# A build-time order that lets buffers of rows sent by POOL be reused only after the landing, and that counts key-value products as traced

## Chip, cores, metric

One core of one Trainium2 chip. The metric is the device time of one execution in microseconds (us). A ratio is the mean time of one kernel's runs over the mean of the other's runs of the same rounds, so it is not quite the ratio of the medians that are quoted.

## The reference

Attention without softmax, then four experts; all float32.

```python
# q, k, v: (8, 8, 576, 64); x: (4608, 512); w1: (4, 512, 1024); w2: (4, 1024, 512)
kv  = np.einsum('bhsd,bhse->bhde', k, v)
out = np.einsum('bhsd,bhde->bhse', q, kv)
rms = np.sqrt(np.mean(out * out, axis=-1, keepdims=True) + 1e-06)
x   = (out / rms * g_norm)            # then (B,H,S,D) -> (B*S, H*D)
p   = domain_probs / (domain_probs.sum(-1, keepdims=True) + 1e-09)
for e in range(4):
    out += p[:, e:e+1] * (np.maximum(x @ w1[e], 0.0) @ w2[e])
```

## The kernel before

The kernel replaces large products by sums and fewer products (Strassen-like forms, two levels deep), so VectorE (DVE) and GpSimd (POOL) make many sums and differences in SBUF while TensorE (PE) multiplies. Rows are worked in 9 chunks for each of the 4 experts. ScalarE (ACT) and DVE take products out of PSUM.

The order of all instructions is made while the kernel is built. A greedy planner holds a model of the time that each operation takes and fills five engines and a stock of buffers ("slots"; the kind "big" has 29, plus 4 that come free later). Each engine then executes its list in order.

```python
def ready(op, eng):                       # may op start on eng, and when
    for d in op.deps:
        when = max(when, d.end + (self.SAME if d.eng == eng else self.CROSS))  # 0.06, 0.3
    ...                                   # need: slots that its outputs want
    for k, n in need.items():
        if len(free[k]) < n + ...: return None
        when = max(when, sorted(free[k])[n - 1][0])
...
    op.start, op.eng = t, eng
    if eng == "SP":                       # loads and plain stores: the landing is counted
        busy[eng] = t + op.cost[eng]
        bus = max(bus, t + 1.5) + op.kb / 215.0
        op.end = bus + 0.5
        ...
    else:                                 # all others, POOL's sends too: over when issued
        op.end = busy[eng] = t + op.cost[eng]
    ...
    for b in op.outs:                     # a slot: the one that came free earliest
        if b.kind is not None and b.slot is None:
            free[b.kind].sort()
            b.slot = free[b.kind].pop(0)[1]
            ...
    for b in op.bufs:                     # the last user of b gives its slot back
        b.left -= 1
        if b.left == 0 and b.kind is not None:
            end = max(o.end for o in [op] + b.readers + b.writers) + self.CROSS
            free[b.kind].append((end, b.slot))
            ...
```

Slots hold the results of one chunk: two "big" buffers `acc`, the first for rows 0 and 1, the second for rows 2 and 3. For the experts after the first, POOL adds them into the output in HBM:

```python
def send(key, i):
    def fn(eng):
        for parts, dst in where:
            if e and not again:
                nc.gpsimd.dma_start(out=dst, in_=cell(i)[parts, :], accum_op=ALU.add)
            else:
                nc.sync.dma_start(out=dst, in_=cell(i)[parts, :])
    plan.add(key, {"POOL": 0.9 * len(where)} if e and not again else {"SP": ...},
             fn, ..., kb=256, holds=[acc[i // 2]])
```

The other users are sums and differences that DVE or POOL may take, whichever is free (`either`), among them the differences `ht` of hidden values that the inner products of a chunk read.

## Time and profile before

| | before |
|---|---|
| time, median of 3 runs | 1790.44 us (1790.4 to 1791.32) |
| traced execution | 1788.53 us, of which 1786.8 from first to last instruction |
| PE busy | 98% |
| idle PE: to 100 / 100 to 640 / 640 to 1715 us / after | 12.9 / 0 / 15.8 / 4.7 us |

How to read it: PE is the bound, so only what makes PE idle counts, and the stretch from 640 us on (experts 2 to 4, the ones that POOL sends) is where it can be helped. The prediction below shows the lines. One it does not show is the chain of work that ended last, by engine:

```profile
PE 85%; DMA 6%; POOL 4%; DVE 2%; issue 2%; SPq 0%; ACT 0%; DVEq 0%; POOLq 0%; ACTq 0%
```

Transfers and POOL hold a tenth of this chain although PE is 98% busy. The chain follows one releaser at a time and credits a transfer with time in which PE still worked.

### The profile page before, as it was taken

The numbers are of one execution on the slowest core, as the hardware profiler recorded it, in microseconds if no ns is written. First come the engines' busy times: TensorE is split into PE (matmuls) and PEld (weight loads), VectorE is DVE, ScalarE is ACT, GpSimd is POOL, SyncE is SP. The second block draws the span as 40 slices with busy tenths as digits, with TensorE's granted clock in tenths as the row PEclk, the third lists the DMA queues.
The fourth block names the chain that finished last, engine by engine and source line by source line (L and its number), as shares of the span: only waits on it lengthen the run. The fifth ranks groups of instructions, "written<-read, shape, count | busy, mean of one in ns | idle before, by whom it ended". The sixth has DMA issues, their size and how long they took to land.

```text
span 1786.8 us, 36290 instructions
## 1 busy us (share of the span) xinstructions
PE 1753.4 (98%) x14132; PEld 1677.8 (94%) x14132; DVE 1140.3 (64%) x1910; ACT 817.5 (46%) x1913; POOL 831.4 (47%) x815
## 2 busy tenths in 40 slices
PE   8899999999999999999999999999999999999998
PEld 8799999999999999999999999999999999999997
DVE  5755564555674667777674577777674577777654
ACT  3544544454343445544443345555543445544541
POOL 4854433444345434444455534444455634444520
PEclk9999999999999999999999999999999999999999
DMA  9744534441443334444464434444465434444441
GB/s 234 243 134 157 173 106 141 157 148 64 153 159 104 106 96 107 107 107 106 120 166 130 107 95 107 107 104 101 106 176 133 115 96 107 107 106 102 103 117 36
DMA packets 148587, 220.79 MB, mean 124 GB/s; under 512 B 49600, under 2 KB 90816, under 8 KB 148416
## 3 DMA queue, kind: packets, MB, share of 16 engines
q1 hardware_dynamic: 133312, 191.21, 33.7%
q0 software_dynamic: 15104, 27.27, 10.7%
q8 instruction: 111, 1.82, 0.4%
q14 instruction: 60, 0.49, 0.1%
HBM read 145.30 MB, written 73.14 MB: 122 GB/s over the span
## 4 chain that ended last, share of the span: by engine, by line
PE 85%; DMA 6%; POOL 4%; DVE 2%; issue 2%; SPq 0%; ACT 0%; DVEq 0%; POOLq 0%; ACTq 0%
PE u L802 38%; PE db L966 18%; PE db L1039 9%; PE ab L1039 8%; PE ab L966 6%; DMA out_dram<-big 4%; POOL big L337 3%; DVE big L337 1%; PE ab L595 1%; PE ab L577 1%; PE ab L605 1%; POOL out_dram L936 1%; PE ab L562 1%; PE ab L644 0%; DMA out_dram<-small 0%
## 5 line engine op out<-in xcount | busy, mean ns | idle before, releaser
L802 PE MATMUL u<-xf,big 128*128 128x128 f32 x3600 | 503.0, 276 | 5.8 <-ACT snap L818 4.7
L826 DVE TENSOR_TENSOR big<-u,snap 128x256 f32<-128x256 f32 x720 | 298.7, 421 | 293.1 <-PE u L802 205.0
L802 PEld LDWEIGHTS u<-xf,big 128*128 128x128 f32 x3600 | 462.2, 192 | 17.1 <-ACT snap L818 7.5
L337 DVE TENSOR_TENSOR big<-big,big 128x1024 f32<-128x1024 f32 (+1 forms) x377 | 431.3, 1159 | 40.4 <-ACT big L785 15.6
L818 ACT ACTIVATE snap<-u 128x256 f32<-128x256 f32 x756 | 289.5, 384 | 362.1 <-PE u L802 263.8
L802 PE MATMUL u<-xf,w1y 128*128 128x128 f32 x2700 | 378.4, 275 | 0.0
L802 PEld LDWEIGHTS u<-xf,w1y 128*128 128x128 f32 x2700 | 340.4, 192 | 2.1
L337 POOL TENSOR_TENSOR big<-big,big 128x256 f32<-128x256 f32 (+1 forms) x174 | 238.3, 1374 | 151.7 <-DVE big L337 65.0
L966 PE MATMUL db<-big,big 128*128 128x256 f32 x1280 | 302.8, 380 | 0.0
L966 PEld LDWEIGHTS db<-big,big 128*128 128x128 f32 x1280 | 231.3, 190 | 25.3
L785 ACT ACTIVATE big<-big 128x1024 f32<-128x1024 f32 x131 | 138.0, 1053 | 38.5 <-DVE big L337 31.8
L818 ACT ACTIVATE big<-u 128x256 f32<-128x256 f32 x240 | 92.1, 384 | 114.6 <-PE u L802 106.8
L1064 ACT ACTIVATE snap<-db 128x256 f32<-128x256 f32 x216 | 76.6, 355 | 125.6 <-PE db L1039 115.3
L337 POOL TENSOR_TENSOR big<-big 128x512 f32<-128x512 f32 (+1 forms) x81 | 95.5, 1184 | 69.0 <-DVE big L337 54.1
L936 POOL DMA_DIRECT2D out_dram<-big x98 | 89.4, 973 | 68.9 <-ACT big L913 50.3
L1072 DVE TENSOR_TENSOR big<-ab,snap 128x256 f32<-128x256 f32 x216 | 83.2, 385 | 51.0 <-PE ab L1039 33.8
L1100 POOL TENSOR_TENSOR big<-big 128x512 f32<-128x512 f32 x21 | 29.6, 1411 | 174.7 <-DVE big L337 174.7
L913 ACT ACTIVATE big<-db,p_all 128x256 f32<-128x256 f32 x100 | 47.4, 474 | 131.5 <-PE db L966 131.5
L920 DVE SCALAR_TENSOR_TENSOR big<-db,p_all,big 128x256 f32<-128x256 f32 x83 | 40.0, 482 | 81.3 <-PE db L966 80.7
L337 POOL TENSOR_TENSOR small<-big,small 128x128 f32<-128x128 f32 (+1 forms) x46 | 28.8, 625 | 127.2 <-DVE big L337 68.0
L1039 PE MATMUL db<-big,big 128*128 128x128 f32 x616 | 86.3, 275 | 0.0
L1039 PE MATMUL ab<-kv,big 128*128 128x128 f32 x500 | 74.7, 278 | 10.1 <-DVE big L1072 10.1
(185 smaller groups left out, 2520.0 us busy)
## 6 DMA issues: line engine op xcount, KB each, us to landing
xf<-x SPq DMA_DIRECT2D x108, 512.0 KB, 3.5
out_dram<-big POOLq DMA_DIRECT2D x82, 256.0 KB, 5.3
xf<-x_h SPq DMA_DIRECT2D x81, 256.0 KB, 3.0
xf<-x SPq DMA_DIRECT2D x81, 256.0 KB, 3.2
x<-xf SPq DMA_DIRECT2D x36, 512.0 KB, 4.5
big<-in_moe_w_dram SPq DMA_DIRECT2D x28, 512.0 KB, 4.4
small<-in_q_dram SPq DMA_DIRECT2D x72, 128.0 KB, 4.4
kv<-in_k_dram SPq DMA_DIRECT2D x30, 288.0 KB, 3.3
```

What stands on the lines that cost most here:

```text
L337: lambda eng: adder(eng).tensor_tensor(out=out_(), in0=a(), in1=b(), op=op),
L785: lambda eng: nc.scalar.activation(out=b.ap[:], in_=b.ap[:], func=ACT.Relu),
L802: nc.tensor.matmul(ps.ap[:, u * P:(u + 1) * P], lhsT=w1f[e][m][mm][1]()[:, u * P:(u + 1) * P], rhs=views[m][mm][1](), start=(mm in (1, 2, ...
L818: lambda eng: nc.scalar.activation(out=where(), in_=ps.ap[:, 0:HN], func=ACT.Copy),
L826: lambda eng: nc.vector.tensor_tensor(out=block(whole, a, t), in0=src.ap[:, 0:HN], in1=add_.ap[:], op=ALU.add),
L913: lambda eng: nc.scalar.activation(out=cell(i, half), in_=ap(), func=ACT.Copy, scale=prob()),
L920: lambda eng: nc.vector.scalar_tensor_tensor(out=cell(i, half), in0=ap(), scalar=prob(), in1=cell(i, half), op0=ALU.mult, op1=ALU.add,),
L936: nc.gpsimd.dma_start(out=dst, in_=cell(i)[parts, :], accum_op=ALU.add)
L966: nc.tensor.matmul(ps.ap[:, 0:HN], lhsT=four(h[m])[:, kt // 2, t, kt % 2, :], rhs=w2f[e][m].ap[:, kt * HN:(kt + 1) * HN], start=(m in (1, ...
L1039: nc.tensor.matmul(ps.ap[:, o * P:(o + 1) * P], lhsT=b.ap[:, col:col + P], rhs=w2q[e][m][mm][1]()[:, kt, :], start=(mm in (1, 2, 5) and o ...
L1064: lambda eng: nc.scalar.activation(out=where(), in_=group_of(ps.ap), func=ACT.Copy),
L1072: lambda eng: nc.vector.tensor_tensor(out=cell(tq, dq), in0=group_of(src.ap), in1=group_of(add_.ap), op=ALU.add,),
```

## The change

Intent: plan the reuse of a sent buffer after its landing (POOL's traced transfers take about 5 us from issue), and give the planner the traced time of the key-value products.

```diff
                     else:
                         op.end = busy[eng] = t + op.cost[eng]
+                        if op.kb:
+                            op.end += 5.5
...
-            plan.add(at(hp), pe(12, D), key_values, reads=[kt, vt], writes=[bank])
+            plan.add(at(hp), {"PE": 0.87}, key_values, reads=[kt, vt], writes=[bank])
```

Only POOL's sends have `kb` on that branch. Nothing that the chip computes changes, only the order of instructions, the choice of engine for some sums and the choice of buffers.

## The prediction

> **What bounds the kernel now.** I read the page's busy shares and its row of slices first, then the engines' busy time by stretch, then the waits and the timeline inside the stretch that is not full.
>
> ```profile
> PE 1753.4 (98%) x14132; PEld 1677.8 (94%) x14132; DVE 1140.3 (64%) x1910; ACT 817.5 (46%) x1913; POOL 831.4 (47%) x815
> ...
> PE   8899999999999999999999999999999999999998
> ```
>
> TensorE (PE, with its weight loads PEld) is the bound from end to end: busy 1753.4 of 1786.8 us. The other engines have a third or more of their time free. Only the 33.4 us in which PE is idle can be won. Where are they?
>
> ```profile
> 0.00:100.00 100.00, 87.10 (x865) 80.60 (x866) 62.39 (x113) 45.63 (x105) 65.66 (x70) 0.97 0.86 228
> 100.00:640.00 540.00, 540.00 (x4089) 499.85 (x4089) 310.94 (x515) 239.35 (x539) 235.40 (x252) 1.00 0.41 133
> 640.00:1715.00 1075.00, 1059.23 (x8792) 1036.38 (x8792) 736.26 (x1233) 514.12 (x1231) 518.66 (x484) 1.00 0.44 113
> 1715.00:1787.00 72.00, 67.05 (x392) 60.94 (x390) 30.67 (x52) 18.44 (x42) 11.68 (x10) 1.00 0.34 74
> ```
>
> After the length of a stretch the columns are the busy times of PE, PEld, DVE, ACT and POOL. Idle PE: 12.9 us in the start-up, none from 100 to 640 (the rest of the first expert, with the attention), 15.8 us from 640 to 1715 (the three experts after it), 5.0 us in the tail. The waits of the third stretch tell what lies behind its 15.8 us:
>
> ```profile
> DVE big L337 <- DMA out_dram<-big: 41.0, 30, 2.5
> ...
> PEld ab L1039 <- DVE big L1072: 12.9, 15, 0.9
> ...
> PE ab L1039 <- DVE big L1072: 10.1, 15, 0.7
> ```
>
> ```profile
> 679.19 0.86 POOL L936 DMA_DIRECT2D out_dram<-big  x1
> ...
> 680.47 1.17 POOL L936 DMA_DIRECT2D out_dram<-big  x1
> ```
>
> ```profile
> 683.83 0.69 DVE L337 TENSOR_TENSOR big<-big 128x512 f32<-128x512 f32 x1 [1.93 <-DMA out_dram<-big]
> ...
> 685.53 0.43 DVE L337 TENSOR_TENSOR big<-big,big 128x256 f32<-128x256 f32 x1 [0.68 <-DMA out_dram<-big]
> ...
> 686.39 0.38 ACT L818 ACTIVATE snap<-u 128x256 f32<-128x256 f32 x1 [2.11 <-DVE big L826]
> ...
> 686.82 0.71 PE L802 MATMUL u<-xf,big 128*128 128x128 f32 x4 [0.17 <-ACT snap L818]
> ...
> 688.24 1.16 PE L1039 MATMUL ab<-kv,big 128*128 128x128 f32 x8 [0.71 <-DVE big L1072]
> ```
>
> (The second wait row is the weight load's own view of the same stops; I do not add it.) This is one event. POOL issues the accumulating sends of two rows of results from one "big" buffer at 679.19 and 680.47. The build-time order counts a send as over when POOL has issued it, so it gives the buffer at once to a DVE subtraction. On the chip that subtraction must wait for the landing: the chain of waits has the second transfer end at 685.44, 4.97 us after its issue. DVE stands still with the evictions of PSUM banks queued behind it, ACT's copy waits for DVE, and PE runs out of free banks twice (0.17 and 0.71 us). I went through all PE gaps of this stretch: 27 gaps in 15 events, and each event has such a DVE wait in the 7 us before its first gap or beside it. 14 of the 15 end with a gap of about 0.7 us on L1039. Five events fall in each of the three experts, about 45 us apart.
>
> **What the Trainium skill says.** "Perfetto Trace Analysis", section "Optimization Strategy", says that the same gap repeating on the engine that should be saturated can mean too little SBUF or PSUM for the next tile. The trace agrees: 15 events of one shape, each on a reused buffer. The same page, "Tensor Engine Instruction", calls ACT, DVE and GPSIMD strict FIFO; the trace agrees, as evictions wait behind the blocked subtraction. It also says there that PE's end times are a model. That matters here: successive 128-column matmuls start 112 ns apart in the trace, yet each is shown as 275 ns long, so a shown gap hides about 0.163 us more of lost start time. "DMA: Bandwidth & Descriptors", section "Anatomy of one DMA", fits a POOL transfer as about 2.0 us plus bytes / 436 GB/s, which would be 2.6 us for 256 KB. The trace differs: 4.9 us median from issue to landing for all POOL sends, 7.8 us at most. I use the trace.
>
> **The change, part by part.**
>
> *Sends.* No instruction, byte or matmul is added or removed. In the build-time order a POOL send now ends 5.5 us after POOL has finished issuing. With 0.9 us modelled for the issue that is 6.4 us from its start, and a reuse follows 0.3 us later. 15 of the 112 landings in the trace are later than 6.4 us, so most reuses, not quite all, are planned late enough. While a slot is missing, the scheduler lets DVE take evictions and other sums first instead of blocking on the subtraction. What is there to win: 15.8 us of shown idle time plus 27 gaps x 0.163 us = 4.4 us, **20.2 us**. (As a cross-check, the start-to-start distances of L802 and L1039 beyond 112 ns sum to 13.1 + 7.3 = 20.4 us in this stretch.) The 41.0 us of DVE waiting are not the gain, as PE covers more than half of them with work that it already has.
>
> What I take off: the planner hands out the slot that became free earliest, so its choice of the slot just sent means that no older "big" slot was free. Holding each acc slot 5.5 us longer makes that shortage real in the plan. The subtractions make forms of h that the inner products consume soon, and a few will come late for PE; landings of over 6.4 us, and drift between planned and real time, leave some DVE waits. I keep three quarters of it, a judgement and not a measurement: 0.75 x 20.2 = **15 us**.
>
> *Key-value products.* They were counted as 2 x 12 x (0.008 + 0.0008125 x 64) + 0.003 = 1.44 us of PE; now 0.87.
>
> ```profile
> 204.10 0.92 PE L577 MATMUL ab<-kv,kv 96*64 96x64 f32 x24
> ```
>
> All 24 matmuls of one pair are shown as 0.92 us long, with a modelled end; the next group starts 0.85 us after them (204.95). So 0.87 is right, and 32 pairs x 0.57 = 18 us disappear from the plan's PE clock, not from the chip's. 21 of the 32 pairs (504 of 768 matmuls) run in the stretch from 100 to 640 where PE is already full: gain 0. Eleven lie in the start-up. There PE waits for loads, attention normalisation and first weight sums; the largest single gap is 4.7 us on a transpose behind a DVE product. A reordering may move this by some 3 us either way: 0 +- 3 us.
>
> *Tail.* Its 5.0 us are the last evictions and sends, by SyncE, and do not change: 0.
>
> Sum: 1790.4 - 15 - 0 - 0 = 1775.4, say **1776 us** (0.8% faster).
>
> **Rivals.**
>
> A. *The wait becomes another wait.* The same shortage of "big" slots now shows as a late operand: fewer DVE waits on transfers, but PE waiting for DVE or POOL sums, or SyncE and the product buffers for slots. For: every event reuses a just-sent slot, so there are no spares at that moment; POOL also waits for DVE for hundreds of us in this stretch, so late sums can propagate. Against: PE may take ready work up to 0.7 of a chunk ahead in the plan, and DVE is busy only 736 of 1075 us. Time: 1785 to 1795 us.
>
> B. *Everything goes through.* All 15 events vanish and nothing replaces them: 1790.4 - 20.2 = 1770 us; with a lucky start-up 1767. PE's own work then leaves no more.
>
> C. *A different order with its own accidents.* A greedy planner that gets other durations changes its order from the first key-value product on, before the sends even begin. It may lengthen the start-up or open a new conflict, such as a load that lands late. For: 12.9 us of start-up idle shows how little it takes. Against: after 100 us PE is full in every stretch without such a send. Time: 1780 to 1800 us.
>
> **Range and chances.** My case (about 60%) is 1771 to 1781; B (15%) is 1767 to 1771; A and C together (25%) are 1781 to 1800. An 8-in-10 range is 1769 to 1788. Faster by over 2% means below 1754.6 us. The floor of B is 1767, so this is all but excluded: 0.01. Slower by over 2% means above 1826 us, which needs a new stall of 36 us that nothing here suggests: 0.02. Within 2%: 0.97.
>
> **What would show it.** In the profile after: DVE waits on transfers of out_dram down from 41.0 us and 30 times to under 10 us; PE's waits on L1072 down from 10.1 us and 15 times to under 3 us; idle PE between 640 and 1715 down from 15.8 to 3 to 6 us; the stretch from 100 to 640 still full; start-up idle 10 to 16 us; busy PE nearly unchanged, 1750 to 1754 us, with 14132 matmuls. The step on the sends is wrong if the DVE waits on transfers vanish while PE idles as long in that stretch behind other releasers (rival A), or if the DVE waits stay (5.5 us too short, or the plan's clock too far from the chip's). The step on the key-value products is wrong if the first 640 us shorten or lengthen by more than 4 us.

## The result and the profile after

| | before | after |
|---|---|---|
| median (range) of 4 runs of the same rounds | 1790.88 (1790.4 to 1796.12) | 1763.97 (1761.96 to 1765.07) |
| ratio, 95% interval | | 0.9842 (0.9821 to 0.9863) |
| traced span | 1786.8 | 1762.9 |

It is 1.6% faster: 27 us where 14.4 was predicted, and below the range.

The page of the kernel after, busy shares, the row of PE's slices and the chain:

```profile
PE 1748.7 (99%) x14152; PEld 1679.4 (95%) x14152; DVE 1126.9 (64%) x1903; ACT 817.7 (46%) x1913; POOL 850.8 (48%) x822
...
PE   9899999999999999999999999999999999999998
...
PE 97%; POOL 1%; DVE 1%; DMA 0%; issue 0%; SPq 0%; ACT 0%; POOLq 0%; DVEq 0%; ACTq 0%
```

Busy time by stretch (length, then busy PE, PEld, DVE, ACT, POOL):

```profile
0.00:100.00 100.00, 90.62 (x892) 84.80 (x893) 63.58 (x113) 45.06 (x105) 63.96 (x68) 0.97 0.88 235
100.00:640.00 540.00, 539.89 (x4087) 499.90 (x4086) 305.47 (x509) 239.23 (x540) 258.54 (x261) 1.00 0.41 132
640.00:1715.00 1075.00, 1075.00 (x8950) 1056.23 (x8950) 738.25 (x1251) 525.03 (x1255) 523.36 (x489) 1.00 0.46 116
```

From 640 to 1715 us PE no longer stops at all: it is busy for all 1075 us, against 1059.23 before. No wait of DVE on a transfer of the output is left. (20 more PE instructions are in this trace; they are warm-up transposes of the start-up.) To place the gain I added up PE's work, each matmul at its usual start distance and without the warm-up, and compared when the same amount of work had been reached in both traces. The kernel after is ahead by 0.45 us at 640 us of before, 8.80 at 900, 16.14 at 1300, 23.86 at 1700 and 23.87 at the end. So 0.45 us come from the start-up, **23.4 us from the fifteen stops**, nothing from the tail.

### The profile page after: what moved, and what is told of

Same layout as the page of the kernel before. It is cut to its first block, busy times and chain, and to the rows that moved or that the text cites. A ratio compares the mean times of both kernels' runs of the same rounds, so it can differ in the third digit from the quotient of the medians.

```text
span 1762.9 us, 36292 instructions
## 1 busy us (share of the span) xinstructions
PE 1748.7 (99%) x14152; PEld 1679.4 (95%) x14152; DVE 1126.9 (64%) x1903; ACT 817.7 (46%) x1913; POOL 850.8 (48%) x822
## 4 chain that ended last, share of the span: by engine, by line
PE 97%; POOL 1%; DVE 1%; DMA 0%; issue 0%; SPq 0%; ACT 0%; POOLq 0%; DVEq 0%; ACTq 0%
PE u L804 44%; PE db L968 18%; PE db L1041 13%; PE ab L1041 10%; PE ab L968 6%; PE ab L597 1%; PE ab L579 1%; PE u L1166 1%; PE ab L607 1%; PE ab L564 1%; POOL rt L516 1%; PE ab L646 0%; POOL big L339 0%; DMA small<-in_q_dram 0%; POOL xf L339 0%; PE db L597 0%
## 5 line engine op out<-in xcount | busy, mean ns | idle before, releaser
L804 PE MATMUL u<-xf,big 128*128 128x128 f32 x3312 | 464.0, 275 | 0.1
L339 DVE TENSOR_TENSOR big<-big,big 128x1024 f32<-128x1024 f32 (+1 forms) x360 | 416.8, 1172 | 28.7 <-ACT big L787 13.6
L804 PEld LDWEIGHTS u<-xf,big 128*128 128x128 f32 x3312 | 426.4, 192 | 7.8 <-ACT snap L820 0.3
L339 POOL TENSOR_TENSOR big<-big,big 128x256 f32<-128x256 f32 (+1 forms) x178 | 249.3, 1405 | 179.6 <-DVE big L339 70.0
L968 PE MATMUL db<-big,big 128*128 128x256 f32 x1336 | 315.8, 380 | 0.0
L968 PEld LDWEIGHTS db<-big,big 128*128 128x128 f32 x1336 | 241.6, 190 | 26.9 <-issue 0.2
L938 POOL DMA_DIRECT2D out_dram<-big x110 | 100.6, 978 | 72.6 <-ACT big L915 54.0
L1074 DVE TENSOR_TENSOR big<-ab,snap 128x256 f32<-128x256 f32 (+1 forms) x204 | 78.9, 387 | 63.1 <-PE ab L1041 39.9
L1041 PE MATMUL db<-big,big 128*128 128x128 f32 x688 | 95.6, 275 | 0.0
L1041 PEld LDWEIGHTS db<-big,big 128*128 128x128 f32 x688 | 86.2, 192 | 0.1
L968 PE MATMUL ab<-big,big 128*128 128x256 f32 x344 | 80.5, 379 | 0.0
```

What stands on the lines that cost most here:

```text
L339: lambda eng: adder(eng).tensor_tensor(out=out_(), in0=a(), in1=b(), op=op),
L804: nc.tensor.matmul(ps.ap[:, u * P:(u + 1) * P], lhsT=w1f[e][m][mm][1]()[:, u * P:(u + 1) * P], rhs=views[m][mm][1](), start=(mm in (1, 2, ...
L968: nc.tensor.matmul(ps.ap[:, 0:HN], lhsT=four(h[m])[:, kt // 2, t, kt % 2, :], rhs=w2f[e][m].ap[:, kt * HN:(kt + 1) * HN], start=(m in (1, ...
L1041: nc.tensor.matmul(ps.ap[:, o * P:(o + 1) * P], lhsT=b.ap[:, col:col + P], rhs=w2q[e][m][mm][1]()[:, kt, :], start=(mm in (1, 2, 5) and o ...
L1074: lambda eng: nc.vector.tensor_tensor(out=cell(tq, dq), in0=group_of(src.ap), in1=group_of(add_.ap), op=ALU.add,),
```

## The experiments

The two halves, both together and a hold of half the length were run first; then, as half did as well as the whole, shorter and longer holds and tests of what in a hold does the work.

### 1. The two halves

```diff
# e1_sends_only            # e2_kv_only
+    if op.kb:              -  pe(12, D)
+        op.end += 5.5      +  {"PE": 0.87}
```

> Only the 5.5 us for POOL sends; key-value products counted as before (1.44 us). Theory L (landings): all of the gain is the fifteen stops of PE behind reused buffers, so this run has no DVE wait on out_dram, no PE idle after 640 us, and is 21 to 26 us faster than before (about 1766 us). Rival R (another order by luck): the gain needs the key-value cost, and this run stays within 10 us of before.

> Only the key-value products at 0.87 us; sends end with their issue as before. Theory L: the fifteen stops stay (DVE waits on out_dram about 41 us, PE idle after 640 us about 16 us), time within 4 us of before (1787 to 1794). Rival R: the new order loses a good part of the stops, at least 8 us faster than before.

> The changed kernel itself, timed in the same rounds as its two halves. About 1764 us, 24 to 27 us faster than before. Theory L: within 4 us of the sends alone. Rival R: at least 10 us faster than the sends alone.

| run | median us | before, same rounds | ratio (95%) |
|---|---|---|---|
| sends only | 1764.61 | 1791.37 | 0.985 (0.9837 to 0.9863) |
| key-value only | 1792.11 | 1791.37 | 0.9997 (0.9983 to 1.001) |
| both (the kernel after) | 1763.65 | 1791.37 | 0.9845 (0.9832 to 0.9858) |

Waits of the run with the key-value cost alone:

```profile
DVE big L337 <- DMA out_dram<-big: 44.3, 30, 2.8
PE ab L1039 <- DVE big L1072: 10.6, 15, 0.7
PE u L802 <- ACT snap L818: 7.7, 12, 2.3
```

Both stops of every event are still there (the last row is PE behind an ACT copy). The sends alone give the gain, the key-value cost alone nothing that can be told from zero; the rival "another order by luck" has fallen for the order that the key-value cost brings (what the order of a hold does is taken up in 2 and 4). The key-value cost does change the plan (its own length falls from 1778.60 to 1764.19 us), but the chip's PE was full there already. That the plan lengths resemble the two measured times is chance: with the sends alone the plan stays 1778.60 us long, while the chip gains all.

### 2. How long must the buffer be held?

`op.end += 2.75`, `+= 0.5`, `+= 0.2`, `+= 8.0` in place of 5.5, key-value cost as before. Holds of 9, 10 and 11 us could not be built: the planner was left with no "big" slot and no operation that could start.

> Sends end 2.75 us after their issue instead of 5.5, key-value products as before. A buffer is then planned free 0.9 + 2.75 + 0.3 = 3.95 us after the start of its last send, some 1.2 us before the landing (5.0 to 5.4 us in the events). Theory L, if the stop of PE grows with the wait of DVE: DVE waits on out_dram 10 to 25 us, PE idle after 640 us 1 to 6 us, time 1767 to 1775. Rival R: time anywhere between before and after, without a link to the DVE waits.

> Sends end 0.5 us after their issue, key-value products as before: the buffer is planned free 1.7 us after the start of its last send, over 3 us before the landing. The build-time plan shows that another big buffer comes free 0.35 us after the one just sent, and that with 0.5 the subtraction takes that other one 0.45 us later. Theory S (a swap: only the order of two free buffers matters): nearly the whole gain, no DVE wait on out_dram, 1764 to 1768 us. Rival W (the hold must cover the landing): most of the wait stays, DVE waits on out_dram over 20 us and time 1775 to 1790.

> Sends end 0.2 us after their issue: in the plan the sent buffer is still the first to be free, by 0.15 us, and the subtraction takes it, behind one other piece of DVE work. Theory S: the stops stay, DVE waits on out_dram 30 to 45 us, time 1785 to 1793. Rival W: a little less waiting than before, in proportion (0.2 of 4 us), so also near before; the two differ by e5 and e6 taken together.

> Sends end 8 us after their issue, the longest hold that I could build in whole microseconds (9 leaves the planner without a buffer). Rival A of the prediction (shortage of buffers comes back as another wait): PE idle after 640 us over 3 us, time 1768 to 1785. If the shortage does not reach PE: 1763 to 1767 us, PE idle after 640 us under 1 us.

| hold, us | median us | ratio to before (95%) | waits of DVE and POOL on output transfers | idle PE, 640 to 1690 us |
|---|---|---|---|---|
| 0 (before) | 1790.4 to 1791.4 | 1 | 42.6 us | 15.8 us |
| 0.2 | 1767.32 | 0.9868 (0.9853 to 0.9883) | 73.1 us | 1.1 us |
| 0.5 | 1765.82 | 0.9858 (0.9843 to 0.9872) | 3.7 us | 0 |
| 2.75 | 1765.36 | 0.9856 (0.9843 to 0.9869) | 0 | 0 |
| 5.5 (sends only) | 1764.61 | 0.985 (0.9837 to 0.9863) | 0 | 0 |
| 8 | 1764.8 | 0.9856 (0.984 to 0.9873) | 0 | 0 |

I missed at 2.75, where I expected a rest of waits, and badly at 0.2, where I expected the stops to stay. The planner's own account of one event (chunk 3 of the second expert; plan times, not the chip's) explains the rest of the table:

```
before: first acc buffer last sent at 733.33, marked free 734.53; taken 734.58 by ht (DVE)
        buffer m13_2 marked free 734.88; taken 738.90 by another ht (POOL)
hold 0.5: acc marked free 735.03; ht takes m13_2's buffer at 735.03; acc taken 738.90 (POOL)
hold 0.2: acc marked free 734.73; ht still takes acc, at 735.03, behind a piece of DVE work
```

Another buffer came free only 0.35 us after the one that had just been sent. Any hold of more than 0.35 us swaps the two. With 0.5 and 2.75 us the sent one is then next needed 5.6 us after its last issue, by POOL, about when it has landed; with 5.5 us it is needed after 6.9 us. Such buffers were there in all fifteen events: when the kernel is built again and its plan printed, a hold of 0.3 us swaps none of the fifteen pairs and one of 0.35 us swaps all.

The run with 0.2 us is the more instructive miss. It still takes the sent buffer, and its engines wait for landings longer than before. Its waits on the output:

```profile
POOL big L339 <- DMA out_dram<-big: 52.0, 13, 4.9
...
DVE big L339 <- DMA out_dram<-big: 20.1, 15, 1.8
```

DVE around the second event, in the kernel before (start, length, what, idle time before it and what ended it):

```profile
725.04 2.04 DVE L337 TENSOR_TENSOR big<-big,big 128x1024 f32<-128x1024 f32 x1
728.93 0.69 DVE L337 TENSOR_TENSOR big<-big 128x512 f32<-128x512 f32 x1 [1.85 <-DMA out_dram<-big]
729.54 0.42 DVE L337 TENSOR_TENSOR small<-big,small 128x256 f32<-128x256 f32 x1
730.28 0.42 DVE L337 TENSOR_TENSOR big<-big,big 128x256 f32<-128x256 f32 x1 [0.32 <-DMA out_dram<-big]
730.62 0.42 DVE L826 TENSOR_TENSOR big<-u,snap 128x256 f32<-128x256 f32 x1
```

and in the run with 0.2 us:

```profile
723.83 1.60 DVE L339 TENSOR_TENSOR big<-big,big 128x1024 f32<-128x1024 f32 x1
725.35 0.41 DVE L339 TENSOR_TENSOR small<-big,small 128x256 f32<-128x256 f32 x1
727.31 0.69 DVE L339 TENSOR_TENSOR big<-big 128x512 f32<-128x512 f32 x1 [1.54 <-DMA out_dram<-big]
727.92 0.42 DVE L339 TENSOR_TENSOR small<-big,small 128x256 f32<-128x256 f32 x1
728.25 0.42 DVE L828 TENSOR_TENSOR big<-u,snap 128x256 f32<-128x256 f32 x1
```

Before, DVE waits for the first landing and then for the second, and only then takes the evictions that PE needs (L826, and L1072 soon after it). With 0.2 us a small difference slips in front of the first wait, and the difference that needs the second landing goes to POOL, which stands for 4 us (52.0 / 13) with nothing behind it that PE misses. (In the event shown the second transfer lands at 728.64 us and POOL goes on at 728.78, after 3.61 us; this wait is put down to a DVE eviction that ended at the same moment, so it is not among the 13.) DVE's one remaining wait of about 1.3 us (20.1 / 15) is nearly always covered. In all, 73 us of waiting go with 1.1 us of shown idle time of PE; the 43 us before went with 15.8.

A hold of 8 us is as good as 5.5: PE idles no time between 640 and 1690 us. So the shortage of buffers that I feared does not reach PE within the range that can be built; it appears at once as a plan that cannot be made.

### 3. Which of the two buffers?

```diff
+    if op.kb and any(x.kind == "big" and x.name[-2:] == "_1" for x in op.bufs):   # e7; "_0": e8
+        op.end += 5.5
```

> 5.5 us only for sends out of the second result buffer of a chunk (rows 2 and 3). In the plan it is taken again 4.6 us after its last issue already before the change. Theory S: no stop comes from it, so time within 4 us of before and DVE waits on out_dram 35 to 48 us. Rival: if both buffers stop DVE, half of the gain, about 1778.

> 5.5 us only for sends out of the first result buffer of a chunk (rows 0 and 1), which the plan of before takes again 1.25 us after its last issue. Theory S: the whole gain, 1763 to 1767 us, DVE waits on out_dram 0 to 5 us. Rival: half of it, about 1778.

Rows 2 and 3 only: 1791.77 us, ratio 1.0011 (0.9993 to 1.0029), with the DVE waits of before. Rows 0 and 1 only: 1765.32 us, ratio 0.9856 (0.9841 to 0.9871), with none. Waits of the run that holds only rows 2 and 3:

```profile
DVE big L339 <- DMA out_dram<-big: 42.4, 30, 2.1
PE ab L1041 <- DVE big L1074: 10.6, 15, 0.7
```

All of the gain lies in one buffer of each chunk, the one that the plan of before takes again 1.25 us after its last issue. The other is taken again after 4.6 us in the plan.

### 4. The same order with another buffer

A hold of half a microsecond or more changes order and buffers together. This run changes the buffer alone: where the earliest free slot is one just sent and the taker is such an `ht` difference, it takes the second in the list. I compared the built programs: on all engines the operations and their output shapes are the same as before, position by position.

```diff
+order = []; sent = set()
...
-    b.slot = free[b.kind].pop(0)[1]
+    b.slot = free[b.kind].pop(int(b.name[:2] == "ht" and b.name[-2:] == "_2"
+                                  and free["big"][0][1] in sent))[1]
...
+    (sent.add if op.kb and eng == "POOL" else sent.discard)(b.slot if b.kind == "big" else -1)
```

> No landing is counted and every engine executes the same operations in the same order as before; the only edit is that a subtraction that would get the buffer just sent takes the next one in the free list. Theory B (the buffer alone makes the stops): the whole gain, 1763 to 1768 us, no DVE wait on out_dram. Theory O (the order that comes with a later end makes it, as the run with 0.2 us suggests): stays near before, 1783 to 1793 us.

1765.74 us, ratio 0.9862 (0.9848 to 0.9877). The same second event:

```profile
724.52 1.57 DVE L337 TENSOR_TENSOR big<-big,big 128x1024 f32<-128x1024 f32 x1
726.12 0.69 DVE L337 TENSOR_TENSOR big<-big 128x512 f32<-128x512 f32 x1
726.73 0.42 DVE L337 TENSOR_TENSOR small<-big,small 128x256 f32<-128x256 f32 x1
727.07 0.42 DVE L337 TENSOR_TENSOR big<-big,big 128x256 f32<-128x256 f32 x1
728.67 0.42 DVE L826 TENSOR_TENSOR big<-u,snap 128x256 f32<-128x256 f32 x1 [1.19 <-PE u L802]
```

The same operations in the same order, without a wait on a landing (5.4 us of such waits are left elsewhere in this run, where I expected none); the eviction now waits for PE and not PE for it. Busy PE from 640 to 1690 us, in the columns of before:

```profile
640.00:1690.00 1050.00, 1049.79 (x8774) 1032.28 (x8773) 724.09 (x1231) 512.57 (x1225) 515.22 (x483) 1.00 0.46 115
```

So the choice of buffer is sufficient with the order left as it was. The run with 0.2 us is its counterpart. In its plan it gives every buffer the same slot as before and differs in the order alone, in 45 places of DVE's list and 15 of POOL's; the holds of 0.5, 2.75 and 5.5 us have its order on every engine, with other buffers. That makes a table of two by two, medians in us:

| | order of before | order of the holds |
|---|---|---|
| sent buffer taken at once | 1790.4 to 1791.4 (before) | 1767.32 (0.2 us) |
| another buffer taken | 1765.74 (this run) | 1764.61 to 1765.82 (0.5 to 5.5 us) |

Either change alone brings nearly all of the gain, and the two do not add up, because either takes the second landing off DVE's path to the next eviction.

No version beats the kernel after: in all that gain, PE idles at most 1.1 us between 640 and 1690 us, and they differ from it by 1 to 4 us. The tests of the hold keep the old key-value cost. Whether that cost brings a microsecond is open: the runs of e3_both (1763.17 to 1764.39) lie just below those of e1_sends_only (1764.41 to 1764.78), but those of the same kernel in the first session spread from 1761.96 to 1765.07.

## Why the prediction was right or wrong

**Right: cause and place.** The fifteen stops from 640 us on, traced back to the reuse of just-sent buffers, are the whole gain (e1 against e2, e8 against e7). The DVE waits on the output fell from 41.0 us to 0, PE's waits on L1072 from 10.1 us to 0, and the stretch from 100 to 640 us stayed full within 0.11 us. Two smaller signs missed: start-up idle was 9.4 us (10 to 16 named) and busy PE 1748.7 us (1750 to 1754), with 20 warm-up transposes more. (The tail's idle time before was 4.7 us, not 5.0: the last window runs past the last instruction.)

**Right: key-value products, start-up and tail at 0 within 3 us.** e2 gives a ratio of 0.9997; the trace puts 0.45 us on the start-up and 0.01 on the tail.

**Wrong: "I keep three quarters of it".** The step before it, "Holding each acc slot 5.5 us longer makes that shortage real in the plan", does not hold. It is true that no older slot was free at that moment. I did not ask when the next one would be: 0.35 us later. The sends' hold did not lengthen the plan by anything (1778.60 us with and without). No sum came late for PE and no DVE wait was left: PE idles 0 us between 640 and 1715, not the 3 to 6 that I named. Kept whole, this term gives 5 us more.

**Wrong: the size of a stop, 20.2 us.** It was 23.4. Shown gaps 15.8 and the hidden 27 x 0.163 = 4.4 were right, but each gap costs a third part: the matmul after it is followed 213 ns later by the next one, not 112 (mean over the 27). That is 27 x 0.101 = 2.7 us, sum 22.9; 0.5 us stay unassigned. The line was in front of me: the first group after a gap is shown as 0.71 us for 4 matmuls, where its neighbours have 0.61. My cross-check of 20.4 us hid the lack because 112 ns is a rounded median: in the kernel after, the mean distance of 128-column matmuls in this stretch is 111.64 ns, and 0.36 ns x 8131 is 2.9 us.

**Not foreseen: the trace of before is a quick execution.** It took 1788.53 us; the medians of before in the later sessions are 1790.4 to 1791.4. With stops, times mostly scatter more: before 1789.9 to 1793.7 in 11 runs, e2 1788.1 to 1794.7 in 6 and e7 1789.3 to 1796.0 in 4, against 0.4 to 1.8 us from lowest to highest in the test runs without stops (3.1 in the four runs of the result). In the trace of e2 the same stops cost 6.4 us more than in that of before, one of them is shown as 2.3 us long. That this scatter comes from the landing times is likely but was not tested. It adds 2 to 3 us to what a trace can promise. The three terms (5 + 3.2 + 2 to 3), the start-up's 0.45 and the rounding of 1775.4 to 1776 make up 11 to 12 us of the 12 that I was off.

**The rivals.** B ("everything goes through") was right with a floor of 1767 that was 3 us too high, for the two reasons just given. A (another wait takes its place) is refuted by e1 and by the hold of 8 us. C (new conflicts from a changed order, 1780 to 1800 us) did not come: e2, whose order changes from the first key-value product on, has the ratio 0.9997.

**"5.5 us, so most reuses are planned late enough".** Harmless as a step, but not the reason. In the trace after, 18 of the 112 landings are later than the 6.4 us planned (15 before), and nothing waits for them. Half a microsecond does it here. I still hold the landing to be the more robust number to give the planner, a judgement and not a test: half a microsecond works by the luck of this plan, in which another buffer was about to come free.

## What to carry to other kernels

When an in-order engine waits for a buffer that is still being sent, ask first which other buffer comes free next: a planner that takes the earliest free one by a margin of 0.35 us, fifteen times over, cost the bound engine 23 us here, where a swap cost nothing. Judge a wait by what stands behind it on its engine, not by its length: POOL stood four microseconds at a time and cost little; DVE stood for two in front of an eviction, and PE stopped. And when sizing stops of PE, compare start distances before, at and after the gap with their mean, not with a rounded median.

## What the Trainium skill lacked or had wrong

- "DMA: Bandwidth & Descriptors", section "Anatomy of one DMA": its fit gives 2.6 us for 256 KB on the POOL path. The 96 accumulating sends of 256 KB in the trace before, often two in flight, took 5.3 us from issue to landing in the median (3.5 to 7.8); the prediction's 4.9 also counts 16 sends of 128 KB. The section gives no figure for accumulation into HBM.
- "Perfetto Trace Analysis", section "Optimization Strategy": a repeated gap may mean too few buffers. Here the gap repeated fifteen times and the count of buffers was enough; the wrong one of two nearly simultaneous ones was taken (e9 removes the gaps with the same count and the same order). The section does not name this case.
- "Perfetto Trace Analysis", section "Tensor Engine Instruction", says that PE's shown ends are a model, but not what a gap then costs. Here 27 gaps shown as 15.8 us cost 23.4: each hid 0.163 us before its first matmul and 0.101 us after it, and 0.5 us stay unassigned.
